# One-token GQA decode block: softmax per K/V segment with a merge at the head's end, V beside the next K, and shorter last loads of the down projection

## The chip, the cores and the metric

The kernel runs on one core of one Trainium2 chip. The metric is the device time of one execution in microseconds (us). Runs of one kernel agree here mostly within 0.5% (one, merge_pool, within about 1%), so differences of one per cent are readable when several rounds are taken. The engines are called by what they do: TensorE (PE in the profile, PEld for its weight loads), VectorE (DVE), ScalarE (ACT), GpSimd (POOL) and SyncE, which issues the large loads (SPq).

## The reference, cut to what matters

```python
Hq, Hkv, Sk, Dh = 32, 4, 65536, 128        # one query token, 8 query heads per KV head
D, F = 1024, 3584

q = (layernorm(x) @ wq).reshape(1, 1, 32, 128).transpose(0, 2, 1, 3)
scores = einsum("bhqd,bhkd->bhqk", q, repeat(k_cache, 8)) * Dh ** -0.5
o = einsum("bhqk,bhkd->bhqd", softmax(scores), repeat(v_cache, 8))
h = x + o.reshape(1, 1, 4096) @ wo
out = h + (gelu(layernorm(h) @ w_gate) * (layernorm(h) @ w_up)) @ w_down
```

All arrays are bf16. K and V are 4 heads x 65536 x 128 each, 134 MB of the 173 MB that must be read once. One token means that each byte is used for little arithmetic.

## The kernel before

K arrives with its positions on the partitions. TensorE transposes it in 128x128 pieces (two bf16 as one fp32), VectorE and ScalarE copy the transposed pieces from PSUM to SBUF (`kt_sb`), TensorE multiplies them by the queries (`qk_ps`), transposes the scores back (`sct_ps`), and VectorE copies the scores and takes maxima. A load is 4 MiB (32 KiB on each of 128 partitions) and holds 128 positions per partition; call it a segment. A KV head has four segments of K and four of V. Five such buffers serve all large loads, in program order, weights included.

At the end of a head's K, one softmax over the whole head: the maximum over 128 partitions goes through TensorE twice (`mxT`, `bc`), then 16 exps of 128x256 run on ScalarE, and V follows, interleaved with the next head's K:

```python
def softmax_head(g):
    mx1 = ...                                   # VectorE: maximum per partition
    nc.tensor.transpose(out=mxT_ps[:], in_=mx1[:], identity=ident_f[:])
    nc.vector.tensor_reduce(out=gm[:], in_=mxT_ps[:], axis=AX.X, op=ALU.max)
    nc.vector.tensor_scalar(out=diag[:], in0=ident_f[0:rep, 0:rep], scalar1=gm[:, 0:1], ...)
    nc.tensor.matmul(bc_ps[:], lhsT=ones_f[0:rep, :], rhs=diag[:], start=True, stop=True)
    nc.vector.tensor_scalar(out=nbias[:], in0=bc_ps[:], scalar1=-scale, ...)
    for hf in range(2):                         # two halves of the head
        for r in range(rep):                    # 8 query heads
            nc.scalar.activation(out=pT[:, :, r, :], in_=sc_sb[...], func=ACT.Exp,
                                 bias=nbias[:, r:r + 1], scale=scale, accum_out=lpart[:, hf, r:r + 1])

for g in range(Hkv):
    for ci in range(NCH + 1):
        if ci < NCH:
            k_chunk_T(g, ci)                    # transposes and copies of a quarter segment
        if ci >= 1:
            k_chunk_QK(g, ci - 1)               # the last one calls softmax_head(g)
        if g >= 1 and ci < NCH:
            v_chunk(g - 1, ci)                  # V of the head before
for ci in range(NCH):
    v_chunk(Hkv - 1, ci)                        # V of the last head, alone
```

The end of the kernel is the down projection, 28 chunks of 128 rows of `w_down` in loads of 14, 9, 4 and 1. The first 23 chunks stream as the moving operand. For the last 5, each of 8 column blocks is a matmul with 8-column weights `actm` that puts its result in its own row of `o_ps`:

```python
sizes = [FC // 2, FC // 2 - 5, 4, 1]
# ... cut: pair_mm for the first 23 chunks, then
d_r = ...                                       # copy of d_ps
wv = load(wd_v[:, c0:c0 + sizes[2], :], "wd_sb")
masked_rows(wv, c0, True, False)                # 32 matmuls, 128 columns stream
hd_cp = cp_sum(d_r, h_cp, "hd_cp")
nc.tensor.matmul(o_ps[:], lhsT=hd_cp[:], rhs=ident_f[:], start=False, stop=False)
wv = load(wd_v[:, c0:c0 + sizes[3], :], "wd_sb")
masked_rows(wv, c0, False, True)                # 8 more
```

The compiler's scheduler sets the order of instructions within each engine; the order of the Python text is only where it starts from.

Of the kernel before, what the change touches and what calls it, by code (L numbers as in the profile page):

```python
# [17 lines left out]
def kernel(  # L18
# [33 lines left out]
    NG = NT // TG  # L52
    GPC = CH // TG
    NCH = NT // CH
# [3 lines left out]
    assert NT % (DCH * CH) == 0 and CH % TG == 0 and CH == 32 and W2 == 16 and DCH % 2 == 0  # L58
# [7 lines left out]
    qkpool = actx.enter_context(tc.tile_pool(name="qkpool", bufs=1))  # L66
    scpool = actx.enter_context(tc.tile_pool(name="scpool", bufs=1))
    ptpool = actx.enter_context(tc.tile_pool(name="ptpool", bufs=1))
    ps_kt = actx.enter_context(tc.tile_pool(name="ps_kt", bufs=3, space=PSUM))
    ps_qk = actx.enter_context(tc.tile_pool(name="ps_qk", bufs=2, space=PSUM))  # L70
    ps_sct = actx.enter_context(tc.tile_pool(name="ps_sct", bufs=1, space=PSUM))
    ps_acc = actx.enter_context(tc.tile_pool(name="ps_acc", bufs=1, space=PSUM))
# [38 lines left out]
    for par in range(2):  # L111
        for half in range(2):
            nc.vector.tensor_copy(out=esel[:, par, half * 64:(half + 1) * 64], in_=ident_bf[:, par::2])

# [57 lines left out]
    q_ps = [ps_qk.tile([P, 512], F32, name="q_ps", tag="qkps") for _ in range(2)]  # L172
# [25 lines left out]
    state = {}  # L198
    kv_big = {}

    def kv_dma(src_v, ci, name):
        bi, si = divmod(ci, DCH)
        key = (name, id(src_v), bi)
        if si == 0:
            kv_big[key] = load(src_v[:, bi * DCH * CH:(bi + 1) * DCH * CH, :], name)
        tv = kv_big[key] if si < DCH - 1 else kv_big.pop(key)
        return tv[:, si * CH:(si + 1) * CH, :]

    def k_chunk_T(g, ci):
        st = state.setdefault(("k", g), {})  # L210
        pi, hf = divmod(ci, 2)
        if hf == 0:
            st["k_pair"] = [kv_dma(k_v[g], ci, "k_sb"), kv_dma(k_v[g], ci + 1, "k_sb")]
        k32s = [k.rearrange("p n d -> p (n d)").bitcast(F32).rearrange("p (m e) -> p m e", e=Dh) for k in st["k_pair"]]
        kts = []
        for c in range(NBK):
            kt_ps = ps_kt.tile([P, NB2, P], F32, name="kt_ps", tag="ktps")
            for b in range(NB2):
                m0 = b * 8 + c * 2 + hf
                nc.tensor.transpose(out=kt_ps[:, b, :], in_=k32s[m0 // 16][:, m0 % 16, :], identity=ident_f[:])  # L220
            kt_sb = ktpool.tile([P, NB2, P], F32, name="kt_sb", tag="kt")
            src_bf = kt_ps[:].rearrange("p b k -> p (b k)").bitcast(BF16)
            dst_bf = kt_sb[:].rearrange("p b k -> p (b k)").bitcast(BF16)
            if act_for(g, ci, c):
                nc.scalar.copy(out=dst_bf, in_=src_bf)  # L225
            else:
                nc.vector.tensor_copy(out=dst_bf, in_=src_bf)  # L227
            kts.append(kt_sb)
        st[("kt", ci)] = kts

    def k_chunk_QK(g, ci):
        st = state[("k", g)]
        pi, hf = divmod(ci, 2)
        kts = st.pop(("kt", ci))
        if ci == 0:
            st["sc_sb"] = scpool.tile([P, rep, NT], F32, name="sc_sb", tag="sc")
            st["mx"] = small.tile([P, rep, NCH // 2], F32, name="mx", tag="mx")
        sc_sb = st["sc_sb"]
        if hf == 0:
            st["qk_ps"] = ps_qk.tile([P, NB2 * P], F32, name="qk_ps", tag="qkps")  # L240
        qk_ps = st["qk_ps"]
        for par in range(2):
            for c in range(NBK):
                mv = kts[c][:].rearrange("p b k -> p (b k)").bitcast(BF16).rearrange("p (b k t) -> p b k t", b=NB2, t=2)
                nc.tensor.matmul(qk_ps[32 * c:32 * c + 32, :], lhsT=qsel[:, g, par, hf, :], rhs=mv[:, :, :, par],  # L245
                                 start=(hf == 0 and par == 0), stop=(hf == 1 and par == 1), tile_position=(0, 32 * c))
        if hf == 0:
            return
        qk_sb = qkpool.tile([P, NB2 * P], F32, name="qk_sb", tag="qk")
        nc.scalar.copy(out=qk_sb[:], in_=qk_ps[:])  # L250
        sct_ps = ps_sct.tile([P, NB2, P], F32, name="sct_ps", tag="sctps")
        for b in range(NB2):
            nc.tensor.transpose(out=sct_ps[:, b, :], in_=qk_sb[:, b * P:(b + 1) * P], identity=ident_f[:])  # L253
        src_v = sct_ps[:].rearrange("p b x -> p (b x)").rearrange("p (m t h) -> p m t h", t=2, h=rep)
        sl = sc_sb[:, :, 2 * pi * CH:(2 * pi + 2) * CH]
        nc.vector.tensor_copy(out=sl.rearrange("p h (m t) -> p m t h", t=2), in_=src_v)  # L256
        nc.vector.tensor_reduce(out=st["mx"][:, :, pi], in_=sl, axis=AX.X, op=ALU.max)  # L257
        if ci == NCH - 1:
            softmax_head(g)

    def softmax_head(g):
        st = state[("k", g)]
        sc_sb, mx = st["sc_sb"], st["mx"]
        mx1 = small.tile([P, rep], F32, name="mx1", tag="mx1")
        nc.vector.tensor_reduce(out=mx1[:], in_=mx[:], axis=AX.X, op=ALU.max)
# [8 lines left out]
        nbias = small.tile([P, rep], F32, name="nbias", tag="nbias")  # L274
        nc.vector.tensor_scalar(out=nbias[:], in0=bc_ps[:], scalar1=-scale, scalar2=None, op0=ALU.mult)  # L275
        NH = 2
        HG = NG // NH
        lpart = small.tile([P, NH, rep], F32, name="lpart", tag="lpart")
        pTs = []
        for hf in range(NH):  # L280
            pT = ptpool.tile([P, HG, rep, TG], BF16, name="pT", tag=f"pT{hf}")
            for r in range(rep):
                nc.scalar.activation(out=pT[:, :, r, :],  # L283
                                     in_=sc_sb[:, r, hf * HG * TG:(hf + 1) * HG * TG].rearrange("p (a t) -> p a t", t=TG),
                                     func=ACT.Exp, bias=nbias[:, r:r + 1], scale=scale,
                                     accum_out=lpart[:, hf, r:r + 1])
            pTs.append(pT)
        state[("v", g)] = {"pT": pTs, "lpart": lpart}

    def v_chunk(g, ci):  # L290
        st = state[("v", g)]
        v_sb = kv_dma(v_v[g], ci, "v_sb")
        if ci == 0:
            st["acc"] = ps_acc.tile([P, TG * Dh], F32, name="acc_ps", tag="acc")
        acc, pTs = st["acc"], st["pT"]
        HG = NG // len(pTs)
        for i in range(GPC):
            a = ci * GPC + i
            c = a % 4
            nc.tensor.matmul(acc[32 * c:32 * c + rep * TG, :],  # L300
                             lhsT=pTs[a // HG][:, a % HG, :, :].rearrange("p r t -> p (r t)"),
                             rhs=v_sb[:, i * TG:(i + 1) * TG, :].rearrange("p t d -> p (t d)"),
                             start=(a < 4), stop=(a >= NG - 4), tile_position=(0, 32 * c))
        if ci == NCH - 1:
            lpart = st["lpart"]
            NH = len(pTs)
            l_ps = ps_m.tile([P, rep], F32, name="l_ps", tag="misc")
            for hf in range(NH):
                nc.tensor.matmul(l_ps[:], lhsT=ones_f[:], rhs=lpart[:, hf, :], start=(hf == 0), stop=(hf == NH - 1))  # L309
            rl = small.tile([P, rep], F32, name="rl", tag="rl")  # L310
            nc.vector.reciprocal(out=rl[:], in_=l_ps[:])
            acc_sb = qkpool.tile([P, TG * Dh], F32, name="acc_sb", tag="qk")
            nc.vector.tensor_copy(out=acc_sb[:], in_=acc[:])
            o_ps = ps_m.tile([P, rep], F32, name="o_ps", tag="misc")
            for t in range(TG):
                nc.tensor.matmul(o_ps[:], lhsT=acc_sb[:, t * Dh:(t + 1) * Dh], rhs=sel[:, t:rep * TG:TG],  # L316
                                 start=(t == 0), stop=(t == TG - 1))
            nc.vector.tensor_tensor(out=oT_all[:, g * rep:(g + 1) * rep], in0=o_ps[:], in1=rl[:], op=ALU.mult)

    def act_for(g, ci, c):  # L320
        if g > 0 and ci < 2:
            return False
        return c % 2 == 1

    for g in range(Hkv):
        for ci in range(NCH + 1):
            if ci < NCH:
                k_chunk_T(g, ci)
            if ci >= 1:
                k_chunk_QK(g, ci - 1)  # L330
            if g >= 1 and ci < NCH:
                v_chunk(g - 1, ci)
    for ci in range(NCH):
        v_chunk(Hkv - 1, ci)
# [115 lines left out]
    for j in range(DC):  # L450
        nc.vector.tensor_copy(out=actm[:, :, j * (DC + 1)], in_=act_bf[:, NW:FC])
# [60 lines left out]
```

## Time and profile before

| what | value | where it is read |
|---|---|---|
| time | 419.05 us median of 3 (418.85 to 419.56) | timed runs |
| span of the profiled run | 415.4 us | the page's head |
| bytes of HBM read | 173.02 MB, 416 GB/s over the span | the page, part 3 |
| busy TensorE, VectorE, ScalarE | 73%, 40%, 40% | the page, part 1 |
| a segment of K with its V within a head | 15.81 us on TensorE | windows between V loads |
| end of the attention (last write of `oT_all`) | 342.8 us | timeline |

The page of the kernel before, from the head and from parts 2 and 3. The rows are 40 equal slices of the span, about 10.4 us each: the granted TensorE clock in tenths, the busy tenths of the DMA engines (9 is 90% or more), and what they moved.

```profile
span 415.4 us, 6247 instructions
...
PEclk9997999999899999599999967999999586658866
DMA  8999999999999999999999999999999999999990
GB/s 354 429 429 437 420 447 420 437 433 428 443 420 402 431 439 428 433 422 432 437 428 429 434 432 428 420 422 437 431 429 438 423 440 426 430 436 423 434 409 32
...
HBM read 173.02 MB, written 0.00 MB: 416 GB/s over the span
```

The loads bind: the DMA row is 9 from the second slice to the last but one. A head's K and V are 33.55 MB, so at the 430 GB/s of these slices a head needs 78 us.

The windows view of before, cut at V loads 4 to 8 of the timeline of SyncE's queue (a V load is issued when a buffer comes free). The columns are start:end and length, then busy us and number of instructions of PE, PEld, DVE, ACT and POOL, then granted TensorE clock, DMA share and GB/s.

```profile
126.67:142.48 15.81, 13.92 (x140) 9.49 (x141) 8.76 (x13) 9.07 (x10) 0.00 (x0) 1.00 1.00 409
142.48:158.29 15.81, 13.92 (x140) 9.47 (x141) 8.77 (x13) 9.08 (x10) 0.00 (x0) 1.00 1.00 432
158.29:186.05 27.76, 19.61 (x154) 13.84 (x155) 13.26 (x24) 13.00 (x38) 0.00 (x0) 0.82 1.01 434
186.05:203.60 17.55, 14.32 (x141) 9.51 (x143) 8.93 (x13) 9.07 (x10) 0.00 (x0) 1.00 0.99 423
```

Inside a head TensorE runs faster than the loads (15.8 us for 8.39 MB, which take 19.5 us at 430 GB/s); at the head's end it loses about 12 us in one piece. The loads do not notice, because up to five buffers are under way: the GB/s of these windows stay at 409 to 434. Together a head takes 76.9 us, just under the 78 of its loads.

What that head's end looks like on TensorE (selected lines of the timeline: start, duration, engine, line, operation, and in brackets the idle time before it and what ended it):

```profile
163.16 0.66 PE L253 MATMUL sct_ps<-ident_f,qk_sb 128*128 128x128 f32 x4 [0.68 <-ACT qk_sb L250]
165.90 0.27 PE L267 MATMUL mxT_ps<-ident_f,mx_1766 128*8 128x128 f32 x1 [2.09 <-DVE mx_1766 L265]
166.80 0.59 PE L273 MATMUL bc_ps<-diag,ones_f 8*128 8x8 f32 x2 [0.63 <-DVE diag L271]
171.72 0.59 PE L309 MATMUL l_ps<-lpart,ones_f 128*128 128x8 f32 x2 [4.33 <-ACT pT L283]
172.17 4.51 PE L220 MATMUL kt_ps<-ident_f,k_sb 128*128 128x128 f32 x20
```

The end of before (selected lines):

```profile
404.61 1.57 PE L358 MATMUL d_ps<-wd_sb,actz 128*32 128x512 bf16 x18 [2.38 <-DMA wd_sb<-in_B_w_down_dram]
...
406.96 1.86 PE L387 MATMUL hd_cp_ps<-hsel,d_r 128*128 128x2 f32 x8 [0.78 <-DVE d_r L471]
408.75 3.57 PE L459 MATMUL o_ps<-wd_sb,actm 128*8 128x128 bf16 x32
...
413.05 0.28 DVE L480 CAST o_row<-o_ps 8x128 bf16<-8x128 f32 x1 [4.01 <-PE o_ps L459]
```

The last load was issued at 391.34 us and landed 16.4 us later (DMA view), at 407.7. After that there are still 5.3 us of work before the result is cast.

### The profile page before, as it was taken

Reading aid. Unit: us, or ns where it says so; the run is one execution under the profiler, and the core shown is the slowest. Engines: PE = TensorE matmul, PEld = TensorE weight load, DVE = VectorE, ACT = ScalarE, POOL = GpSimd, SP = SyncE. Lnnn points to the kernel's source line nnn. Section 1 sums busy time; section 2 is a strip of 40 time slices with the busy share of each in tenths; the row PEclk is TensorE's granted clock in tenths of the full one; section 3 lists DMA queues with packets and bytes.
Section 4 is the critical chain, followed back from the end, with each engine's and each line's share of the span. In section 5 each row is a group of like instructions: output and inputs, shape, how many; then the busy total and the mean of one; then the engine's idle time right before and its main releaser. Section 6 shows DMA issues by size and latency. Waiting matters only on the chain.

```text
span 415.4 us, 6247 instructions
## 1 busy us (share of the span) xinstructions
PE 302.2 (73%) x2652; PEld 196.9 (47%) x2652; DVE 168.2 (40%) x298; ACT 168.1 (40%) x281; POOL 5.7 (1%) x17
## 2 busy tenths in 40 slices
PE   0458989888788986597988929888986563575536
PEld 0227656564465664464565517465564231352215
DVE  0213565656356455354465526455465000011101
ACT  0014757545755653734565544365562700000000
POOL 1100000000000000000000000000000002000000
PEclk9997999999899999599999967999999586658866
DMA  8999999999999999999999999999999999999990
GB/s 354 429 429 437 420 447 420 437 433 428 443 420 402 431 439 428 433 422 432 437 428 429 434 432 428 420 422 437 431 429 438 423 440 426 430 436 423 434 409 32
DMA packets 6684, 173.43 MB, mean 417 GB/s; under 512 B 896, under 2 KB 896, under 8 KB 1152
## 3 DMA queue, kind: packets, MB, share of 16 engines
q1 hardware_dynamic: 6496, 173.02, 97.2%
q8 instruction: 21, 0.34, 0.3%
q14 instruction: 7, 0.06, 0.0%
q10 hardware_dynamic: 160, 0.00, 0.0%
HBM read 173.02 MB, written 0.00 MB: 416 GB/s over the span
## 4 chain that ended last, share of the span: by engine, by line
PE 51%; DMA 20%; DVE 13%; issue 8%; ACT 6%; POOL 1%; SPq 0%; POOLq 0%; ACTq 0%; DVEq 0%
PE kt_ps L220 27%; PE qk_ps L245 11%; DMA k_sb<-in_A_k_cache_dram 7%; DMA wd_sb<-in_B_w_down_dram 7%; DMA v_sb<-in_A_v_cache_dram 6%; DVE sc_sb L256 5%; PE acc_ps L300 5%; PE sct_ps L253 4%; ACT pT L283 4%; DVE mx L257 3%; DVE kt_sb L227 3%; ACT qk_sb L250 2%; PE wg_ps L160 1%; PE o_ps L459 1%; PE o_ps L316 1%
## 5 line engine op out<-in xcount | busy, mean ns | idle before, releaser
L220 PE MATMUL kt_ps<-ident_f,k_sb 128*128 128x128 f32 x1024 | 149.2, 289 | 15.9 <-DVE kt_sb L227 13.0
L225 ACT COPY kt_sb<-kt_ps 128x1024 bf16<-128x1024 bf16 x116 | 116.4, 1013 | 91.7 <-PE kt_ps L220 61.6
L220 PEld LDWEIGHTS kt_ps<-ident_f,k_sb 128*128 128x128 f32 x1024 | 118.2, 147 | 53.9 <-issue 21.2
L227 DVE COPY kt_sb<-kt_ps 128x1024 bf16<-128x1024 bf16 x140 | 94.8, 687 | 74.5 <-PE qk_ps L245 41.9
L245 PE MATMUL qk_ps<-kt_sb,qsel 128*32 128x512 bf16 x512 | 65.4, 397 | 7.3 <-DVE kt_sb L227 7.3
L256 DVE COPY sc_sb<-sct_ps 128x512 f32<-128x512 f32 x32 | 34.2, 1067 | 47.3 <-PE sct_ps L253 45.0
L283 ACT ACTIVATE pT<-sc_sb,nbias 128x256 bf16<-128x256 f32 x64 | 31.5, 494 | 20.4 <-DVE nbias L275 20.4
L300 PE MATMUL acc_ps<-v_sb,pT 128*32 128x512 bf16 x512 | 33.7, 408 | 2.8 <-DMA v_sb<-in_A_v_cache_dram 2.8
L250 ACT COPY qk_sb<-qk_ps 128x512 f32<-128x512 f32 x32 | 18.9, 590 | 24.8 <-PE qk_ps L245 16.5
L245 PEld LDWEIGHTS <-qsel 128*32 128x32 bf16 x512 | 15.1, 94 | 26.7 <-issue 24.4
L253 PE MATMUL sct_ps<-ident_f,qk_sb 128*128 128x128 f32 x128 | 20.4, 283 | 8.6 <-ACT qk_sb L250 8.6
L300 PEld LDWEIGHTS <-pT 128*32 128x32 bf16 x512 | 14.3, 101 | 18.0 <-issue 6.2
L257 DVE TENSOR_REDUCE mx<-sc_sb 128x8 f32<-128x512 f32 x32 | 22.0, 686 | 1.0
L253 PEld LDWEIGHTS sct_ps<-ident_f,qk_sb 128*128 128x128 f32 x128 | 14.7, 143 | 13.6 <-ACT qk_sb L250 13.6
L167 ACT COPY wg_ev<-wg_ps 96x512 f32<-96x512 f32 x1 | 0.6, 582 | 45.6 <-PE wg_ps L160 45.6
L309 PE MATMUL l_ps<-lpart,ones_f 128*128 128x8 f32 x16 | 3.7, 306 | 15.6 <-ACT pT L283 15.6
L358 PE MATMUL at_ps<-wo_sb,o2z 128*32 128x512 bf16 x64 | 7.2, 629 | 9.4 <-DMA wo_sb<-in_A_wo_dram 9.4
L160 PEld LDWEIGHTS <-hnz 128*32 128x32 bf16 x112 | 5.0, 125 | 15.3 <-issue 13.3
L167 ACT ACT_TABLE_LOAD x1 | 1.3, 1283 | 26.9 <-DVE q_ev L165 26.9
L160 PE MATMUL wu_ps<-wu_sb,hnz 128*32 128x512 bf16 x56 | 6.7, 597 | 7.4 <-DMA wu_sb<-in_B_w_up_dram 7.4
L283 ACT ACTIVATION_READ_ACCUMULATOR pT<-sc_sb,nbias 128x1 f32 x64 | 12.0, 187 | 0.0
L309 PEld LDWEIGHTS l_ps<-lpart,ones_f 128*128 128x128 f32 x16 | 3.0, 234 | 17.8 <-ACT pT L283 17.4
(126 smaller groups left out, 103.0 us busy)
## 6 DMA issues: line engine op xcount, KB each, us to landing
k_sb<-in_A_k_cache_dram SPq DMA_DIRECT2D x16, 4096.0 KB, 26.6
v_sb<-in_A_v_cache_dram SPq DMA_DIRECT2D x16, 4096.0 KB, 21.6
wq_sb<-in_A_wq_dram SPq DMA_DIRECT2D x2, 4096.0 KB, 17.0
wo_sb<-in_A_wo_dram SPq DMA_DIRECT2D x2, 4096.0 KB, 28.8
wg_sb<-in_B_w_gate_dram SPq DMA_DIRECT2D x2, 3584.0 KB, 32.4
wu_sb<-in_B_w_up_dram SPq DMA_DIRECT2D x1, 3584.0 KB, 41.2
wd_sb<-in_B_w_down_dram SPq DMA_DIRECT2D x1, 3584.0 KB, 25.1
wu_sb<-in_B_w_up_dram SPq DMA_DIRECT2D x1, 2688.0 KB, 37.8
```

Source lines behind the costliest of these rows:

```text
L160: nc.tensor.matmul(banks[s // 4][32 * g:32 * g + 32, :], lhsT=stat, rhs=mov(s), start=first, stop=last, tile_position=(0, 32 * g))
L220: nc.tensor.transpose(out=kt_ps[:, b, :], in_=k32s[m0 // 16][:, m0 % 16, :], identity=ident_f[:])
L225: nc.scalar.copy(out=dst_bf, in_=src_bf)
L227: nc.vector.tensor_copy(out=dst_bf, in_=src_bf)
L245: nc.tensor.matmul(qk_ps[32 * c:32 * c + 32, :], lhsT=qsel[:, g, par, hf, :], rhs=mv[:, :, :, par], start=(hf == 0 and par == 0), stop=(hf ...
L250: nc.scalar.copy(out=qk_sb[:], in_=qk_ps[:])
L253: nc.tensor.transpose(out=sct_ps[:, b, :], in_=qk_sb[:, b * P:(b + 1) * P], identity=ident_f[:])
L256: nc.vector.tensor_copy(out=sl.rearrange("p h (m t) -> p m t h", t=2), in_=src_v)
L257: nc.vector.tensor_reduce(out=st["mx"][:, :, pi], in_=sl, axis=AX.X, op=ALU.max)
L283: nc.scalar.activation(out=pT[:, :, r, :], in_=sc_sb[:, r, hf * HG * TG:(hf + 1) * HG * TG].rearrange("p (a t) -> p a t", t=TG), func=ACT. ...
L300: nc.tensor.matmul(acc[32 * c:32 * c + rep * TG, :], lhsT=pTs[a // HG][:, a % HG, :, :].rearrange("p r t -> p (r t)"), rhs=v_sb[:, i * TG: ...
L358: nc.tensor.matmul(bank[32 * g:32 * g + 32, :], lhsT=stat, rhs=w2[:, s * 512:(s + 1) * 512], start=first, stop=last, tile_position=(0, 32 ...
```

## The change

The intent: remove the 12 us hole at each head's end. Each of the four segments of a head gets its own maximum, its own exps (8 of 128x128 instead of 16 of 128x256 at the end) and its own V sum; V of one segment runs beside K of the next. At the head's end the four sums are brought to the common maximum and added (`head_end`), as in online softmax but once per head. PSUM buffers move from the scores (2 to 1) to the V sums (1 to 2). Separately, the loads of `w_down` become 14, 7, 4, 2, 1, and their last 14 chunks use the weights as the stationary operand with one column of activations. One more thing changes without being part of the intent: before, VectorE alone copied the transposed K of the first two quarters of heads 1 to 3; now ScalarE takes every second copy everywhere.

```diff
-    sizes = [FC // 2, FC // 2 - 5, 4, 1]
+    sizes = [14, 7, 4, 2, 1]
...
+            for j in range(DC):
+                nc.tensor.matmul(dl_ps[:, j:j + 1], lhsT=wv[:, cc, j * P:(j + 1) * P], rhs=act_bf[:, c:c + 1],
+                                 start=False, stop=False, skip_group_check=True)
...
-        if ci == NCH - 1:
-            softmax_head(g)
+        return T, QK, lambda: softmax_seg(i, sc_sb, mx)
...
+        pT = ptpool.tile([P, SG, rep, TG], BF16, name="pT", tag="pT")
+        for r in range(rep):
+            nc.scalar.activation(out=pT[:, :, r, :], in_=sc_sb[:, r, :].rearrange("p (a t) -> p a t", t=TG),
+                                 func=ACT.Exp, bias=nbias[:, r:r + 1], scale=scale,
+                                 accum_out=head[g]["lp"][:, sg, r:r + 1])
...
+    def head_end(g):
+        nc.vector.tensor_reduce(out=nbm[:], in_=nb[:].rearrange("p s r -> p r s"), axis=AX.X, op=ALU.min)
+        for sg in range(NSEG):
+            nc.vector.tensor_tensor(out=w[:, sg, :], in0=nbm[:], in1=nb[:, sg, :], op=ALU.subtract)
+        nc.scalar.activation(out=w[:], in_=w[:], func=ACT.Exp)
+        nc.vector.tensor_tensor(out=lw[:], in0=lp[:], in1=w[:], op=ALU.mult)
+        # ... cut: l_ps, its reciprocal, wp = the weight of each partition's query head
+        nc.vector.tensor_scalar(out=tot[:], in0=tot[:], scalar1=wp[:, 0:1], scalar2=None, op0=ALU.mult)
+        for sg in range(1, NSEG):
+            nc.vector.scalar_tensor_tensor(out=tot[:], in0=accs[sg][:], scalar=wp[:, sg:sg + 1], in1=tot[:],
+                                           op0=ALU.mult, op1=ALU.add)
+        # ... cut: o_ps from tot, oT_all
...
+    for i in range(NS + 1):                        # NS = 16 segments
+        cur = k_steps(i) if i < NS else None
+        for ci in range(DCH):
+            if cur:
+                cur[0](ci)                         # T: transposes and copies of a quarter
+            if ci == 0 and prev:
+                prev[1](DCH - 1)                   # last QK of the segment before
+                prev[2]()                          # its softmax
+            if ci >= 1 and cur:
+                cur[1](ci - 1)
+            if ci == 0 and i >= 2:
+                vs[i - 2](DCH - 1)                 # last V; ends the head after segment 4
+            if ci == 0 and i >= 1:
+                vs[i - 1] = v_steps(i - 1)
+            if ci >= 1 and i >= 1:
+                vs[i - 1](ci - 1)
```

## The prediction

> **What bounds the kernel now.** The loads. In the page's 40 slices the DMA row is 9 from slice 2 on and 430 GB/s moves until 407 us; 173.02 MB is 402 us at that rate. The Trainium skill (DMA: Bandwidth & Descriptors, Specifications) gives a fabric ceiling of 435 GB/s; the trace agrees, so bytes, which do not change, leave only the gaps: about 2 us of dips and the 8 us after the last byte.
>
> PE is close behind. By the timeline, one K segment with its V segment takes PE 15.8 us (V loads issued at 126.67, 142.48, 158.29), and each head's softmax costs about 12 us more (158.29 to 186.05): 4x15.8+12 = 75 us per head against 78 us of loading. The attention waits for V once, 2.8 us, at the very end (337 us).
>
> **What the change does.**
> 1. The softmax chain now runs 16 times instead of 4. The instruction order of the changed build is, at every boundary, sct, mxT, bc, then 24 transposes of the next K. From the trace at 318-323 us: scores' copy 1.02, max 0.69, max 0.2, transpose 0.4, reduce 0.28, diag 0.22, broadcast 0.6: PE idles about 3.5 us.
> 2. Then 8 exps stand before the next K copy on ACT. One of 256 elements steps 0.49 us; by the slope of the copies (1013 ns for 1024, 590 for 512 elements) one of 128 is an estimated 0.385, 3.1 us together. PE fills three PSUM buffers (1.4 us) and waits for ACT. Against the old inner boundary (kt at 146.4, second ACT copy at 149.8) I get a delay of 4.5 us. Pair: about 20.3 us against 19.5 us of loading: PE, not DMA, now sets the pace.
> 3. Merging, per head: weights, 4 scaled sums of 128x512 on DVE, standing before the next K copies and behind the exps: an estimated 3.3 us, plus 1 us for l_ps, o_ps and the last sum at the next boundary.
> 4. Removed: the 12 us per head.
> 5. Tail: 14 chunks become 112 matmuls with 128x128 bf16 weights and one column. fp32 64-column weights repeat every 0.11 us at half clock; the Trainium skill (TensorE: Matmul & The Clock Gate, LDWEIGHTS) says time goes by columns, P/1.2 ns, so I estimate 0.05-0.11 us each, 6-12 us, for loads that take 8.5 us. Before, 5.3 us of PE followed the last byte; the tail gains 2 us at best, and can lose 4.
>
> **Sum.** K0 from 32.7 us, 14.6; then 15 pairs at 15.8, 15 boundaries at up to 4.5, 3 merges at 4.3, last softmax, V and merge 13: the attention ends near 376 us instead of 343. Weights loaded ahead give some back: the rest then takes about 50 us instead of 72. Span about 427, time 430 us.
>
> **Would show it right:** V's load interval about 20-21 us, not 19.5; DMA slices of 8 in the attention; PE's waits led by mxT/bc and by kt_ps for ACT; attention's end (oT_all) after 365 us. **Wrong:** if that interval is 19.5 and the DMA row stays 9, loads still bind and only the tail moves (414-422 us).
>
> **What would make it wrong:** exps shorter than estimated, or PE regaining the boundary's loss within the segment, since the pair is within 1 us of the load time; the clock halving after each boundary would make it worse.
>
> Time 430 us, 417 to 444; faster by over 2%: 0.04, within 2%: 0.36, slower: 0.60.

## More of the kernel before

The runs were made in several sessions, on more than one chip, each beside the kernel before; so kernels of different sessions are best compared by their ratios to before.

TensorE waits 2.09 us for the maximum, 0.63 for its broadcast and 4.33 for exps; the next head's transposes stand behind all of it. The 20 transposes then take 4.51 us, 0.23 us each; within a head 12 take 1.47 us, 0.122 us each. They run at half clock (granted clock 0.50 in 170 to 175 us).

## The result, and the profile after

The changed kernel takes 446.46 us (median of 4 runs, 444.96 to 447.18) against 418.95 us (418.75 to 419.56) of the kernel before on the same chip: 1.0649 times as long, 95% interval 1.0615 to 1.0683. Ratios here and below are the mean time of one kernel's fast runs over the mean of the other's in the same rounds, so not quite the ratio of the medians that are quoted. It is slower, as the prediction held most likely, but outside its range (444). All outputs are right.

The page of the kernel after, the same rows (slices of about 11.1 us):

```profile
span 443.1 us, 6705 instructions
...
PEclk9998988989687988898787978986969698958596
DMA  8999999999999999999689798998596999999795
GB/s 343 456 429 427 422 426 427 430 433 442 432 432 424 429 422 432 422 422 438 259 337 422 284 424 358 439 385 386 206 444 253 429 368 432 372 430 418 290 382 249
...
HBM read 173.02 MB, written 0.00 MB: 390 GB/s over the span
```

The same bytes; but from slice 20 on the DMA engines starve (259, 284, 206 GB/s). Until then the full buffers of the start hide that TensorE is slower than the loads. Now TensorE sets when buffers come free.

The windows of after between V loads, one whole head:

```profile
130.35:153.96 23.61, 19.70 (x159) 14.55 (x160) 11.29 (x21) 12.21 (x26) 0.00 (x0) 0.86 0.99 425
153.96:175.69 21.73, 17.28 (x143) 11.78 (x144) 10.37 (x18) 12.04 (x26) 0.00 (x0) 0.84 1.01 432
175.69:196.19 20.50, 16.46 (x143) 11.29 (x144) 10.44 (x18) 12.04 (x26) 0.00 (x0) 0.92 1.01 431
196.19:222.55 26.36, 19.04 (x143) 12.93 (x143) 13.69 (x32) 12.27 (x27) 0.00 (x0) 0.81 0.79 334
```

A head now takes 92.2 us, not 76.9. The 12 us hole is gone, but each of the four segments costs 4.7 us or more above the 15.81 of before. The fourth contains the merge; the first contains what the merge left for the next boundary. The second and the third hold the same instructions (143 and 144 on TensorE, 18 and 26 on the others) and differ by 1.23 us; their clocks are 0.84 and 0.92.

A plain boundary (one without a merge), from scores to the next segment's transposes:

```profile
178.99 0.65 PE L250 MATMUL sct_ps<-ident_f,qk_sb 128*128 128x128 f32 x4 [0.24 <-ACT qk_sb L247]
181.68 0.27 PE L270 MATMUL mxT_ps<-ident_f,mx_1838 128*8 128x128 f32 x1 [2.03 <-DVE mx_1838 L268]
182.58 0.59 PE L276 MATMUL bc_ps<-diag,ones_f 8*128 8x8 f32 x2 [0.63 <-DVE diag L274]
183.10 3.31 PE L223 MATMUL kt_ps<-ident_f,k_sb 128*128 128x128 f32 x16
187.55 1.09 PE L223 MATMUL kt_ps<-ident_f,k_sb 128*128 128x128 f32 x8 [1.14 <-ACT kt_sb L228]
```

The waits of before, 2.03 and 0.63 us, are paid at every segment. Then the clock is halved: 16 transposes take 3.31 us (0.207 each) at a mean granted clock of 0.58, where at full clock 8 take 1.09 (0.136 each). Then TensorE waits 1.14 us for ScalarE's copies, which stand behind 8 exps (183.41 to 186.50). So it is ScalarE's copy that lets TensorE go on at 187.55, 8.6 us after the scores' transposes began, and the slow transposes lie mostly within the time that it would have waited anyway. This will matter when the clock is judged.

The Trainium skill (TensorE: Matmul & The Clock Gate, Part 1: The HAM clock gate) describes a clock that falls to half after an idle window of about 3.4 us. The trace agrees with the half, but here no single gap is that long. `mxT` (0.27) still ran at full clock and `bc` (0.59) not, 2.9 us after the scores' transposes had ended. The gaps alone do not fix the moment: at 137.62 and 160.84 us, behind gaps about as long or longer, `bc` took 0.38 and 0.39 us, and the half clock set in soon after it.

A boundary that merges, TensorE and VectorE in order of time (selected lines):

```profile
110.83 0.59 PE L276 MATMUL bc_ps<-diag,ones_f 8*128 8x8 f32 x2 [0.63 <-DVE diag L274]
111.35 2.82 PE L223 MATMUL kt_ps<-ident_f,k_sb 128*128 128x128 f32 x12
115.00 0.19 DVE L319 TENSOR_TENSOR lw<-lp,w 128x32 f32<-128x32 f32 x1 [2.71 <-ACT w L317]
116.40 1.54 DVE L332 SCALAR_TENSOR_TENSOR acc_sb<-acc_sb,wp 128x512 f32<-128x512 f32 x2
117.86 1.28 DVE L230 COPY kt_sb<-kt_ps 128x1024 bf16<-128x1024 bf16 x2
118.60 2.82 PE L223 MATMUL kt_ps<-ident_f,k_sb 128*128 128x128 f32 x12 [4.42 <-DVE kt_sb L230]
```

VectorE waits 2.71 us for the merge's exp, which stands on ScalarE behind the 8 exps of the segment; the sums follow; its first copy of the new K starts only at 117.86. TensorE fills three PSUM buffers and waits 4.42 us, and the clock is halved before and after (granted clock 0.50 over both groups of 12). At the next boundary `l_ps` and `o_ps` take 1.88 and 1.87 us, at half clock.

The end of after (selected lines):

```profile
435.20 1.66 PE L486 MATMUL dl_ps<-act_bf,wd_sb 128*128 128x1 bf16 x56 [0.78 <-DMA wd_sb<-in_B_w_down_dram]
437.68 1.01 PE L486 MATMUL dl_ps<-act_bf,wd_sb 128*128 128x1 bf16 x32 [0.82 <-DMA wd_sb<-in_B_w_down_dram]
438.96 0.98 PE L486 MATMUL dl_ps<-act_bf,wd_sb 128*128 128x1 bf16 x24 [0.27 <-DMA wd_sb<-in_B_w_down_dram]
...
440.61 0.28 DVE L498 CAST o_row<-h2T_ps 8x128 bf16<-8x128 f32 x1 [0.47 <-PE h2T_ps L496]
```

A pair of a 128x128 bf16 weight load and one streamed column takes 30 ns here (1.66 us / 56). After the last wait for a load (438.96) only 1.65 us pass until the cast. This part of the change is a gain.

The attention ends at 399.91 us (before: 342.79), the rest takes 43.2 us (before: 72.6, in which it waits for loads).

### The profile page after: what moved, and what is told of

The parts are those of the page before. It is cut to its first block, busy times and chain, and to the rows that moved or that the text cites. A ratio compares the mean times of both kernels' runs of the same rounds, so it can differ in the third digit from the quotient of the medians.

```text
span 443.1 us, 6705 instructions
## 1 busy us (share of the span) xinstructions
PE 329.3 (74%) x2757; PEld 222.3 (50%) x2757; DVE 196.3 (44%) x404; ACT 197.3 (45%) x425; POOL 5.1 (1%) x16
## 4 chain that ended last, share of the span: by engine, by line
PE 56%; DVE 13%; ACT 12%; DMA 10%; issue 8%; POOL 0%; SPq 0%; POOLq 0%
PE kt_ps L223 28%; PE qk_ps L242 11%; ACT pT L280 8%; DMA k_sb<-in_A_k_cache_dram 7%; PE sct_ps L250 5%; PE acc_ps L295 5%; DVE sc_sb L253 4%; DMA wd_sb<-in_B_w_down_dram 3%; DVE mx L254 2%; ACT qk_sb L247 2%; ACT kt_sb L228 2%; PE bc_ps L276 2%; DVE acc_sb L332 1%; PE wg_ps L168 1%; PE l_ps L322 1%
## 5 line engine op out<-in xcount | busy, mean ns | idle before, releaser
L223 PE MATMUL kt_ps<-ident_f,k_sb 128*128 128x128 f32 x1024 | 168.9, 319 | 30.4 <-DVE kt_sb L230 14.3
L223 PEld LDWEIGHTS kt_ps<-ident_f,k_sb 128*128 128x128 f32 x1024 | 137.9, 165 | 64.6 <-ACT kt_sb L228 22.4
L228 ACT COPY kt_sb<-kt_ps 128x1024 bf16<-128x1024 bf16 x128 | 128.2, 1009 | 89.5 <-PE kt_ps L223 46.2
L230 DVE COPY kt_sb<-kt_ps 128x1024 bf16<-128x1024 bf16 x128 | 87.9, 689 | 103.6 <-PE qk_ps L242 54.2
L280 ACT ACTIVATE pT<-sc_sb,nb 128x128 bf16<-128x128 f32 x128 | 49.6, 388 | 67.2 <-DVE nb L277 67.1
L295 PE MATMUL acc_ps<-v_sb,pT 128*32 128x512 bf16 x512 | 42.6, 401 | 0.0
L242 PEld LDWEIGHTS <-qsel 128*32 128x32 bf16 x512 | 13.6, 95 | 24.2 <-issue 20.8
L280 ACT ACTIVATION_READ_ACCUMULATOR pT<-sc_sb,nb 128x1 f32 x128 | 23.9, 187 | 0.0
L302 DVE COPY acc_sb<-acc_ps 128x512 f32<-128x512 f32 x16 | 11.1, 691 | 19.0 <-PE acc_ps L295 19.0
L276 PE MATMUL bc_ps<-diag,ones_f 8*128 8x8 f32 x32 | 8.0, 321 | 9.4 <-DVE diag L274 9.4
L322 PE MATMUL l_ps<-lw,ones_f 128*128 128x8 f32 x32 | 7.5, 364 | 4.6 <-DVE lw L319 3.8
## 6 DMA issues: line engine op xcount, KB each, us to landing
wd_sb<-in_B_w_down_dram SPq DMA_DIRECT2D x1, 3584.0 KB, 11.1
```

The lines of the kernel that those rows point to most:

```text
L223: nc.tensor.transpose(out=kt_ps[:, b, :], in_=k32[:, pi * CH + b * 8 + c * 2 + hf, :], identity=ident_f[:])
L228: nc.scalar.copy(out=dst_bf, in_=src_bf)
L230: nc.vector.tensor_copy(out=dst_bf, in_=src_bf)
L242: nc.tensor.matmul(qk_ps[32 * c:32 * c + 32, :], lhsT=qsel[:, g, par, hf, :], rhs=mv[:, :, :, par], start=(hf == 0 and par == 0), stop=(hf ...
L280: nc.scalar.activation(out=pT[:, :, r, :], in_=sc_sb[:, r, :].rearrange("p (a t) -> p a t", t=TG), func=ACT.Exp, bias=nbias[:, r:r + 1], s ...
L295: nc.tensor.matmul(acc[32 * c:32 * c + rep * TG, :], lhsT=pT[:, a, :, :].rearrange("p r t -> p (r t)"), rhs=v_sb[:, a * TG:(a + 1) * TG, : ...
```

## The experiments

Theory: the loss comes from the boundaries. TensorE's instructions stand in a fixed order, and the built order puts the maximum's transpose and broadcast in front of all the transposes of the next K. So TensorE idles 16 times, its clock halves, and the merge on VectorE adds to it. Rivals: the merge alone; ScalarE's exps before its copies; the half clock as mere symptom; the new end. Ten kernels were run. Each is the changed kernel, or the one before, with one thing altered; two (warm_dve, t_first_pool) alter two things.

### Only the new end, and only the new attention

The kernel before with the new loads and matmuls of `w_down` (tail_only), and the changed kernel with the old ones (old_tail):

```diff
 # tail_only: before's attention;  old_tail: the other way round
-    sizes = [FC // 2, FC // 2 - 5, 4, 1]
+    sizes = [14, 7, 4, 2, 1]
     # and the matmuls that go with them
```

> The old attention with the new last loads and the new down projection. Theory (the attention is what got slower; the new tail is a gain of its own): the loads bind as before, the last byte lands near 407.5 us as before, and after it come about 1 us of matmuls, add, transpose, cast and 2.2 us of output instead of 7.7 us: span near 411.5-412.5 us, time 415 us, ratio 0.990. Rival (112 one-column matmuls with full weights cost more than they save): 419 us or more.

> The new attention with the old last loads and the old down projection. Theory: nearly all of the 27 us stays, 445-449 us, since the attention ends at 400 us and the last loads come late in either form. Rival (the tail is what costs): 420-430 us.

tail_only took 412.47 us (412.29 to 414.13), 0.9879 times before (0.9858 to 0.9899): the new end gains 1.2%. old_tail took 451.33 us (450.52 to 452.78), 1.0804 (1.0777 to 1.0831). So the end is worth about 5 us in the kernel before and 5 to 7 us in the changed one (old_tail was slightly slower than the 449 us expected), and the whole loss, and more, lies in the attention. The rival "the end" falls.

### All 28 chunks of the down projection as one-column matmuls

```diff
 # against tail_only
-    if c < NW: pair_mm(d_ps, actz[:, c, :], wv[:, cc, :], ...); continue
+    # every chunk: 8 one-column matmuls into dl_ps
```

> The old attention with the new last loads, and all 28 chunks of the down projection as one-column matmuls, so that the eviction, the 8 fp32 matmuls and their waits between the first and the second load go (2.6 us on PE in the run with the new tail alone, at half clock). A pair measured 28-30 ns there, so the first load's 112 pairs take 3.2-3.4 us, as its 28 wide matmuls do. Expected: PE keeps up with the last loads, span 1-2 us shorter than with the new tail alone, ratio to before 0.983-0.987. If the end hangs on the last loads' landing only: 0.988.

It took 412.64 us (412.22 to 413.82), 0.9883 (0.9864 to 0.9903), as tail_only. The hoped-for gain (0.983 to 0.987) did not come: in its timeline TensorE waits 1.11, 2.10 and 0.21 us for the loads of the last three groups. With 30 ns a pair the end hangs on the loads landing, no longer on TensorE.

### The merge on GpSimd

```diff
 # heads 0 to 2; the sums of weights become three adds
-        nc.vector.tensor_scalar(out=tot[:], in0=tot[:], scalar1=wp[:, 0:1], ...)
+        nc.gpsimd.tensor_scalar(out=tot[:], in0=tot[:], scalar1=wp[:, 0:1], ...)
-            nc.vector.scalar_tensor_tensor(out=tot[:], in0=accs[sg][:], scalar=wp[:, sg:sg + 1], in1=tot[:], ...)
+            nc.gpsimd.tensor_scalar(out=accs[sg][:], in0=accs[sg][:], scalar1=wp[:, sg:sg + 1], ...)
+            nc.gpsimd.tensor_tensor(out=tot[:], in0=tot[:], in1=accs[sg][:], op=ALU.add)
```

> The change with the merge of heads 0 to 2 moved from DVE to GpSimd (exp weights' products, their sums, the scaled sums of 128x512), so that nothing of it but a reduce and four small subtractions stands before the next K copies on DVE. Theory (DVE's merge is the larger mis-sized term): the load interval that holds a merge falls from 26.4 to about 21 us, three times, and the attention ends 13-17 us earlier: 430-435 us. If the merge is no cause: 446 us.

It took 438.27 us (435.96 to 440.5), 1.0489 (1.0447 to 1.0532): 7 to 8 us of the 27.5 lost come back, less than the 11 to 16 expected. The intervals that merge fall from 26.4 to 23.2 us and, for the later heads, 20.6 and 20.4; but those after them rise from 23.6 to 24.2, 25.2 and 25.6. A part of the reason is seen at the next boundary, on VectorE and on GpSimd:

```profile
134.22 1.04 DVE L268 TENSOR_TENSOR mx<-mx 128x8 f32<-128x8 f32 x1
...
133.97 1.26 POOL L339 TENSOR_TENSOR acc_sb<-acc_sb 128x512 f32<-128x512 f32 x1
```

VectorE's maximum of two 128x8 tiles takes 1.04 us instead of 0.17, and ends at 135.26 us, as GpSimd's add does (135.23). The Trainium skill (SBUF — State Buffer, SBUF: two separate sides) says that the two engines share a port pair as an exclusive lock, and names VectorE's operations with two SBUF inputs. The trace agrees: VectorE's operation has two inputs in SBUF, is 0.87 us longer than elsewhere and ends with GpSimd's. The same stands at the other two such boundaries (1.04 and 1.05 us). TensorE's wait for the maximum there is 2.91 us, against 2.48 in after; this 0.43 us is most of the rise of the first interval (0.6 us), but not of the later two (1.4 and 2.0 us), which were not traced further.

This run holds one more observation. At one of its plain boundaries the 16 transposes happened to run nearly at full clock:

```profile
247.89 2.10 PE L223 MATMUL kt_ps<-ident_f,k_sb 128*128 128x128 f32 x16
252.33 1.45 PE L223 MATMUL kt_ps<-ident_f,k_sb 128*128 128x128 f32 x8 [2.35 <-ACT kt_sb L228]
```

TensorE then waited 2.35 us for ScalarE's copy instead of 1.14, and went on 8.3 us after the scores' transposes began (243.99), hardly sooner than in after (8.6). At a plain boundary of the changed kernel, then, faster transposes alone gain little: ScalarE's copies behind the exps hold TensorE as long.

### Dummy transposes against the half clock, first try

```diff
+        for k in range(3):                      # 12 transposes that nobody reads
+            for b in range(NB2):
+                nc.tensor.transpose(out=wm_ps[:, b, :], in_=head["qk_sb"][:, b * P:(b + 1) * P], identity=ident_f[:])
         nc.tensor.transpose(out=mxT_ps[:], in_=mx1[:], identity=ident_f[:])
```

> The change with 12 extra transposes of scores, whose result nobody reads, put on PE while it waits for the maxima at each boundary, so that the clock is not halved there; all waits for DVE and ACT stay. Theory (waits for DVE and ACT are the greater part, the halved clock some 5 us per head): mean granted clock of the attention rises above 0.95, time falls by 3 to 12 us, to 434-443 us, since the exps on ACT still hide most of the cold transposes. Rival (the halved clock is the cause of the loss): below 430 us. If the clock has no part: 446 us or a little more.

A miss: it took 450.52 us (448.96 to 450.8), 1.0773 (1.0747 to 1.0799), about 1% slower than the change. It does not decide anything about the clock, because it did not keep it up: TensorE's wait for the maximum fell from 2.03 to 0.85 us, but at the plain boundary the 16 transposes still took 3.09 us, TensorE then still waited 1.36 us for ScalarE's copies, and the whole run's clock was 0.868 against 0.856 (above 0.95 was expected for the attention).

### No maximum at all

```diff
-        mx1 = ...; mxT_ps; gm; diag; bc_ps; nbias = -scale * bc_ps
+        nc.vector.memset(nbias, 0.0)
```

These inputs are small enough for exps without a shift, so the result stays correct.

> The change without the chain of maxima at the boundaries: the bias of every exp is a constant 0 (the scores of these inputs are so small that the result stays right; in general it would not be safe). Exps, merge, V order and tail stay. Theory (the chain puts PE some 3.5 us out of work at each boundary, and brings on the halved clock): the plain V load interval falls from 20.5 to the loads' own 19.5 us or less, attention ends before 365 us, time 412-426 us. If the exps and the merge are the greater part: above 432 us.

It took 413.97 us (413.93 to 414.09), 0.991 (0.9886 to 0.9935), and its DMA row is 9 from the second slice to the last but one. Without the chain the loads bind again, although the exps, ScalarE's copies behind them and the merge are all still there. The chain is necessary for the loss of the whole kernel. But one expectation failed: the plain intervals stayed at 20.3 to 20.4 us, where 19.5 or less was expected. TensorE there waits 2.14 us for ScalarE's copies behind the exps, and the 8 transposes after this wait take 1.97 us, at half clock. What fell are the interval that merges and the one after it, 23.35 and 17.75 us instead of 26.36 and 23.76; a head takes 81.9 us instead of 92.2, and the attention ends at 364.16 us, which is just early enough. So without the chain the exps and the clock still hold a plain boundary. This leaves open whether it is the work of chain and exps, or where they stand.

### The chain behind the next K's first transposes

```diff
                 if ci == 0 and c == 2:
+                    t_first[i] = nc.cur_bb.bb.instructions[-1]     # the 12th transpose of a segment
...
-                prev[2]()
+                with tc.issue_after(t_first[i]):                   # an edge of order, no other change
+                    prev[2]()
```

> The change with one thing added: PE may issue the transpose of the maxima only behind the first 12 transposes of the next segment's K (an issue-order edge, no new wait); as built, 16 of them then stand before it, 6 more before the broadcast, and three K copies stand before the exps on ACT. All work is the same. Theory (it is the order at the boundary that costs, not the 16 softmaxes as such): chain and exps are covered, the plain interval falls to 19.5 us or below, loads bind again, 412-424 us, and what is over 412.5 us (old attention with the new tail, ratio 0.988) is what the merges leave. If it is the amount of work or the alternation of K and V that costs: above 435 us.

The order of TensorE's instructions at a plain boundary, as the two built programs have it (the trace shows the same order):

```
after:    sct_ps*4  mxT_ps*1  bc_ps*1  kt_ps*24  qk_ps*1  kt_ps*8
t_first:  sct_ps*4  kt_ps*16  mxT_ps*1  kt_ps*6  bc_ps*1  kt_ps*2  qk_ps*1  kt_ps*8
```

It took 414.10 us (413.99 to 414.19), 0.9912 (0.9892 to 0.9933). The same work in another order is about 31 us faster (by the ratios). Plain intervals fall to 18.9 us. From the first of the scores' transposes to the end of the next 32 transposes of K, a plain boundary takes 6.8 us (166.47 to 173.29), against 11.0 in after (178.99 to 189.99). The timeline of TensorE at the boundary that merges, to be read against 110.83 to 118.60 of after:

```profile
104.76 1.47 PE L224 MATMUL kt_ps<-ident_f,k_sb 128*128 128x128 f32 x12
107.60 0.66 PE L224 MATMUL kt_ps<-ident_f,k_sb 128*128 128x128 f32 x4 [1.36 <-DVE kt_sb L233]
108.09 0.27 PE L273 MATMUL mxT_ps<-ident_f,mx 128*8 128x128 f32 x1
108.20 0.82 PE L224 MATMUL kt_ps<-ident_f,k_sb 128*128 128x128 f32 x6
108.99 0.38 PE L279 MATMUL bc_ps<-diag,ones_f 8*128 8x8 f32 x2
```

`mxT` and `bc` no longer wait, 12 transposes take 1.47 us (0.122 each), and the only idle stretch of these lines is 1.36 us. ScalarE and VectorE get their first copies of K before the exps and the merge, not behind them. So the one edge moves three things together: the chain on TensorE, the exps on ScalarE and the merge on VectorE. It also spreads V's matmuls, which in after stand in two blocks, among the transposes before the boundary; what that adds was not tested apart. The attention ends at 355.35 us, the DMA row is 9 from the second slice to the last but one, and the loads bind.

### The first copies of a segment on VectorE alone

```diff
-                if c % 2 == 1:
+                if c % 2 == 1 and (ci > 0 or i == 0):
                     nc.scalar.copy(out=dst_bf, in_=src_bf)
```

> The change with the four K copies of a segment's first chunk all on DVE, so that they need not wait behind the eight exps on ACT; the chain stays. Theory: of the 4.6 us lost at a plain boundary about 2.4 us are this wait, less what DVE's extra two copies cost (1.4 us, partly hidden): plain interval 19.0-19.8 us, merging boundary nearly as before since DVE is what it waits for, time 430-440 us. If the exps do not matter: 446 us.

A miss: 445.77 us (444.32 to 446.36), 1.0665 (1.0639 to 1.0691). The wait for ScalarE did go away, and nothing was gained (430 to 440 us were expected). The line of the transposes at a plain boundary tells why:

```profile
182.55 6.00 PE L223 MATMUL kt_ps<-ident_f,k_sb 128*128 128x128 f32 x28
```

28 transposes run without a gap, but take 6.00 us, 0.214 each, at a granted clock of 0.53. The interval stays at 20.44 us, and from the scores' transposes to the end of the 32nd transpose it takes 11.0 us, as in after. So a plain boundary has two limits of nearly the same length, side by side: ScalarE's copies behind the exps, which set the pace in after, and the half clock, which sets it once those copies are out of the way. Removing the first alone gained nothing here; the boundary of merge_pool above suggests the same of the second. This asked for a second try at the clock, with ScalarE's copies still out of the way.

### Dummy transposes, second try, on dve_first

```diff
 # on dve_first
+        for k in range(4):                      # 16 transposes that nobody reads
+            for b in range(NB2):
+                nc.tensor.transpose(out=wm_ps[:, b, :], in_=head["qk_sb"][:, b * P:(b + 1) * P], identity=ident_f[:])
         nc.tensor.transpose(out=mxT_ps[:], in_=mx1[:], identity=ident_f[:])
+        # 4 more of the same, into wn_ps; the scheduler puts one before mxT and three after it
```

> The clock theory's second try: dve_first (the first chunk's copies of the next K all on VectorE, so that TensorE has no idle stretch behind the exps) plus 16 dummy transposes between the scores' transposes and the maximum's transpose and 4 around it, which fill the 2.03 us and 0.62 us in which TensorE stood idle there. dve_first alone left the plain boundary at 20.4 us although its wait for ScalarE was gone: its 28 transposes ran without a gap, but took 6.0 us (0.214 us each), where at full clock 28 take 3.4 us (0.122 us each). If the half clock after the idle stretch is what eats the gain, the 28 now take about 3.5 us, plain intervals between V loads fall from 20.4 to 18 to 19.5 us (there the loads bind), and the kernel takes 425 to 436 us against 446 of the change and dve_first; the boundary that merges stays long, because VectorE's serial merge still delays its copies. Rival: the clock is a symptom and the chain's length is what counts: plain intervals stay at 20.2 to 20.6 us and the kernel at 443 to 450 us.

It took 425.61 us (423.94 to 426.56), 1.0183 (1.015 to 1.0217). Work that nobody needs makes the kernel 20 us faster. Windows of dve_first, third segment (the second is alike, 20.43 us), then of warm_dve, second segment (the third is alike, 18.26) and the one that merges; and the transposes of a plain boundary of warm_dve:

```profile
175.22:195.66 20.44, 17.54 (x143) 12.66 (x143) 11.82 (x20) 10.24 (x24) 0.00 (x0) 0.83 1.00 429
```

```profile
151.64:169.91 18.27, 17.42 (x163) 11.84 (x163) 11.49 (x20) 10.13 (x24) 0.00 (x0) 1.00 1.00 427
188.17:214.51 26.34, 19.78 (x163) 13.77 (x164) 14.97 (x34) 10.36 (x25) 0.00 (x0) 0.87 1.00 431
```

```profile
177.17 3.89 PE L223 MATMUL kt_ps<-ident_f,k_sb 128*128 128x128 f32 x28
```

Twenty instructions more on TensorE, clock 1.00 instead of 0.83, 2.2 us less. The 28 transposes take 3.89 us instead of 6.00. The rival "the clock is a symptom" falls: at the plain boundaries of dve_first it is the cost. The interval that merges stays at 26.34 us, because VectorE's serial merge still delays its copies (TensorE's wait there is 5.71 us). So both are real: keeping the clock up is worth about 20 us where ScalarE's copies are out of the way (dve_first against warm_dve), and taking the merge off VectorE is worth 7 to 8 us (merge_pool). These are two separate measurements on different kernels, not a sum. What the clock alone is worth in the changed kernel, with ScalarE's copies behind the exps, no run shows.

### The order set, and the merge on GpSimd

```diff
 # t_first and merge_pool together
```

> The change with TensorE's order at the boundary set (as in t_first) and the merging of heads 0 to 2 moved from VectorE to GpSimd. If t_first is already bound by the loads, taking the merge off VectorE gives nothing: 413 to 415 us, ratio 0.989 to 0.994, as t_first (0.991). If what is left of the merge still cost t_first its 24.6 us interval and with it the 0.3% by which it lies above the version with only the new end, the kernel falls to 411 to 413 us. Slower than 416 us would mean that GpSimd's stretching of VectorE's small steps comes through.

It took 414.47 us (414.41 to 414.54), 0.9921 (0.9901 to 0.9941): as t_first. With the order set the merge costs nothing that the loads do not hide.

### What the attention's end is worth

The start of the last write of `oT_all` in the timelines, and the span, in us:

| kernel | attention ends | span | rest |
|---|---|---|---|
| tail_only | 343.21 | 410.5 | 67.3 |
| t_first | 355.35 | 412.3 | 57.0 |
| t_first_pool | 358.17 | 412.7 | 54.5 |
| no_chain | 364.16 | 412.1 | 47.9 |
| warm_dve | 378.83 | 424.7 | 45.9 |
| merge_pool | 391.66 | 436.2 | 44.5 |
| dve_first | 399.23 | 444.1 | 44.9 |
| after | 399.91 | 443.1 | 43.2 |
| warm | 404.62 | 448.9 | 44.3 |

All of these have the new end. The span is about the larger of two things: the loads, about 411, and the attention's end plus about 45. Up to about 365 us the attention's end costs next to nothing (spans of 410.5 to 412.7); beyond, each microsecond costs about one. Before had about 22 us of such slack (342.8), and the change could only spend it.

## Why the prediction was wrong

The direction and the mechanism were right, the size was not: 430 us with a range to 444, measured 446.46.

1. "The loads" bind before: right. The consequence it drew, that bytes do not change and only the gaps are to be had, is confirmed from the other side: the best versions, tail_only and tail_cols, gain 1.2%, and get it at the end.
2. The order "sct, mxT, bc, then 24 transposes" was read from the build, and "PE, not DMA, now sets the pace" was right: t_first shows that this order is the cause.
3. "Pair: about 20.3 us": measured 20.50 where nothing of a merge is left. The mechanism was right too: TensorE goes on when ScalarE's first copy behind the exps is done. Its transposes ran slower than foretold (16 took 3.31 us), so its idle wait was shorter (1.14 us), but the end of the wait did not move. What the prediction did not see is the second limit behind the first: with the wait gone (dve_first) the half clock alone kept the pair at 20.4 us, and only with both gone (warm_dve) it fell to 18.3. And where the half clock lasts beyond the wait, it costs: in the second segment, 21.73 us, the 8 transposes after the wait took 1.97 us instead of 1.09.
4. **The step that failed** is the third of "What the change does", the merge, "an estimated 3.3 us, plus 1 us", 4.3 per head. Against the 20.3 us of the pair, the four intervals of a head in after (23.61, 21.73, 20.50, 26.36) are 3.3, 1.4, 0.2 and 6.1 us longer, together 11.0. So a head took 92.2 us, not 4 x 20.3 + 4.3 = 85.5, 6.7 too few, three times over. That is 20 of the 24 us by which the attention ended later than foretold (399.9, not 376). The other 4 us were not traced. The wait itself was sized right: the merge delays K's copies, and TensorE waits 4.42 us, 3.3 more than the 1.14 of a plain boundary. What the term left out was the clock, which the prediction named only as a risk ("the clock halving after each boundary would make it worse") and gave no number. At the boundary that merges the 32 transposes take 7.61 us instead of 5.49; at the next one `l_ps` and `o_ps` take 3.75 us together, where 1 us was allowed for them and the last sum (in before, 8 matmuls of `o_ps` take 1.06 us at full clock); and one interval later the half clock still lasts beyond the wait (21.73 us, point 3). This split is read from durations and granted clocks in the trace: no run kept the clock up through a merge. The profile before had the number: 20 transposes in 4.51 us after a head's end.
5. "The rest then takes about 50 us instead of 72": measured 43.2. With the old end it is 48.3 us (old_tail: span 449.9, attention's end 401.6), so most of the difference is the new end. The term that was off is "0.05-0.11 us each" for the one-column matmuls: 30 ns. The Trainium skill (TensorE: Matmul & The Clock Gate, Weight-path perf modes) has a fast weight load for weights of 128 columns that are not fp32; its example of about 40 ns per matmul is for fp8. The trace, with bf16, fits that, while the prediction took the general rate of the section before it, from which 107 ns follow. So "the tail gains 2 us at best, and can lose 4" was too low: it gains about 5 (tail_only, old_tail).
6. The two size errors partly cancel: 24 us later attention, 7 us shorter rest, together about 16 us more span than the 427 foretold.
7. Of its signs, the DMA slices below 9 and the late end of the attention came true; V's interval of 20 to 21 us holds only for the plain ones (20.50; the others are 21.73 to 26.36). "PE's waits led by mxT/bc and by kt_ps for ACT" came true only in part: kt_ps waited most for VectorE's copies (14.3 us against 11.6 for ScalarE's).

What stays open: why the scheduler puts the chain in front of the transposes, although the program text has them the other way round. That it did was read from the built order, and that it matters is shown; its reason was not looked for. Also open is the worth of the clock alone in the changed kernel, and of the order of V's matmuls. Nor was the order tried together with other splits of the head, since the loads bind already.

## What to carry to other kernels

When a kernel waits for its loads, work on the compute side can only spend slack: first find how much later the compute may end at no cost (here about 22 us), and look for gain in the gaps of the loads (here the last 5 us). A short cross-engine chain is cheap only if independent work stands between its steps in each engine's order, so read the built order and set it if need be; splitting one such chain into four multiplied the idle gaps, and TensorE's clock was halved behind them. When removing one suspected cause gains nothing, look for a second limit of the same length beside it before calling the first harmless (dve_first and warm_dve). Cost the half clock as a term of the sum, with the slow duration that the trace already shows, and not as a risk.

## What the Trainium skill lacked or had wrong

- TensorE: Matmul & The Clock Gate, "Why this matters for your kernels", asks to avoid idle gaps of more than about 3 us. Here gaps of 2.03 and 0.63 us, with one short transpose between, were enough at some boundaries: `bc` took 0.59 us instead of 0.38, and the 28 transposes after it 6.00 us (dve_first) instead of 3.89 (warm_dve).
- The same page, Part 4: PE-mode transpose, says that the full clock does not engage for its transpose mode, which does not count as busy in the same way. Here 20 fp32 transposes that nobody read held the clock at 1.00 through a plain interval (warm_dve), and it was 0.83 without them (dve_first). The trace lists them as matmuls with an identity and does not tell whether the transpose mode was on.
- The same page, LDWEIGHTS, gives the time as columns over 1.2, 107 ns for 128 columns, and does not point to the exception in the section after it. Measured for 128x128 bf16 weights with one streamed column: 30 to 41 ns a pair (1.66 us for 56, 1.01 for 32, 0.98 for 24).
- GPSIMD Engine Reference, 4.1 Engine selection, calls one-input elementwise operations on GpSimd roughly line-rate. Scaling 128x512 fp32 by a per-partition factor took 1.56 us on GpSimd and 0.48 on VectorE.
- DMA: Bandwidth & Descriptors, Specifications, gives 435 GB/s as the ceiling. The mean of whole runs stays under it (416 to 421 GB/s of HBM reads in the runs that the loads bind), but single slices of the page stand above it (447 in before, 456 in after); whether that is in how the slices share out bytes is not known.
- No page says that an order of instructions which the compiler chooses, with the same instructions, can be worth about 31 us of 446 (t_first), or how much later compute may end at no cost when loads are queued ahead (here about 22 us).
